# A spectral-mixing kernel with its rows re-tiled so that every output DMA spans 128 partitions, and its last mode split over two PSUM banks

## The chip, the core and the metric

The kernel runs on one core of a Trainium2 chip. A core has five engines that run side by side: TensorE (PE, with weight loads, PEld, shown apart), VectorE (DVE), ScalarE (ACT), GpSimd (POOL) and SyncE (SP), and 16 DMA engines that move data between HBM and the on-chip memory SBUF. SBUF and PSUM, where matmuls accumulate, have 128 partitions. The metric is the device time of one execution in microseconds; lower is better.

## What is computed

Linear attention over 8 batches, 8 heads, 576 rows and head size 64, then a mixing of the rows in the Fourier domain with one pair of 512x512 weight matrices for each of 64 modes, and a channel product with a ReLU:

```python
def phi(x):  return np.where(x > 0, x, np.exp(x) - 1.0) + 1.0
q_p, k_p = phi(q), phi(k)
kv  = np.einsum('bhsd,bhse->bhde', k_p, v)
num = np.einsum('bhsd,bhde->bhse', q_p, kv)
den = np.einsum('bhsd,bhd->bhs', q_p, np.sum(k_p, axis=2))[..., None] + 1e-06
x   = (num / den).transpose(0, 2, 1, 3).reshape(B, S, H * D)   # 8 x 576 x 512

X = np.fft.rfft(x, axis=1)[:, :64]
Y[:, :64] = X * (w_r + 1j * w_i)       # per mode m: a 512x512 complex product
u = x + np.fft.irfft(Y, n=S, axis=1)
out = u + np.maximum(u @ w_ch, 0.0)    # float32
```

The weights are 128 matrices of 1 MB each, so most of the bytes that are read are weights. The output has 8 x 576 x 512 numbers of 4 bytes, 9.44 MB.

## The kernel before

The 576 rows of a batch are cut into four main tiles of 128 rows and a tail of 64; two batches' tails share one tile. Thus there are 36 tiles, t = 0 to 35. The kernel has three stages.

First, for each batch, q, k and v are loaded with a partition holding 9 consecutive rows (s = 9 p + j), phi is applied, and q is transposed on TensorE. The transposes for the nine j go to PSUM in an order that makes four tiles of 128 columns, and ScalarE copies them to `qT`:

```python
for sl in range(NJ):                                    # NJ = 9, NP = 64
    j = 8 if sl == 8 else 4 * (sl % 2) + sl // 2
    nc.tensor.transpose(qT_ps[:, sl]..., phi["q", b][:, hpp, j]..., id16)
nc.scalar.copy(out=qT[:, hpp].rearrange("p t (j r) -> p t j r", r=NP),        # L231
               in_=qT_ps.rearrange("p j t r -> p t j r"))
...
def num_matmuls(num, orow, qT, kv_sb, jj, pinned=False):
    cols = slice(jj * 128, min(jj * 128 + 128, NJ * NP))
    ...  nc.tensor.matmul(num[hpo][orow, c0:c0 + 65],                         # L158
                          qT[rows, hpp, h2, cols], kv_sb[rows, hpp, h2, :])
```

So partition p of tile jj holds row 9 p' + jj (first 64 partitions) or 9 p' + 4 + jj (second 64). The Fourier constants are built for this order. A transform of x gives the modes (L295, weights `x16[:, jj, dc::4]`).

Second, the weights stream in, and each mode is a product over four column groups of the array, a copy out of PSUM, and a pick of the rows (L372):

```python
def mode_product(kk, ps, stage, yt_ps):
    wr, wi = w_get(kk)
    P = ps.tile([128, D], F32, tag="P", bufs=2)
    for dc in range(NDC): nc.tensor.matmul(P[quad, :], xt_cols(dc, 1, kk), wr[:, dc, :], ...)  # L354
    if kk >= NM - 4: keep_warm(6)
    for dc in range(NDC): nc.tensor.matmul(P[quad, :], xt_cols(dc, 0, kk), wi[:, dc, :], ...)  # L362
    st = stage.tile([128, D], F16, tag="ystage", bufs=2)
    (VectorE for even kk, else ScalarE): copy st <- P                                          # L368, L370
    for ec in range(NDC): nc.tensor.matmul(yt_ps[:, ec, kk % 8, :], st[...], pick_sb)          # L372
```

Beside it, `channel_product` forms x again for each tile (L158 once more), and `form_rows` makes Y and Z = Y w_ch for the first 56 modes (L490, L494).

Third, when the last mode is there, Z and y of the last eight modes are formed, sent to the other batches' tiles by small DMAs, and each tile gets its inverse transform (L517), ReLU on ScalarE (L547), the addition on VectorE (L553) and its output DMA:

```python
for ec in range(NDC): nc.tensor.matmul(z_ps, rows[ec], wch16[:, ec, :], ...)      # L603
for ec in range(NDC): nc.tensor.transpose(y_ps[:, ec, :], rows[ec], id16)         # L605
nc.scalar.copy(out=last[:, 1, 0:hw], in_=z_ps[:, 0:hw])                           # L607
nc.vector.tensor_copy(out=last[:, 1, hw:D], in_=z_ps[:, hw:D])                    # L608
nc.vector.tensor_copy(out=last[:, 0, :], in_=y_ps...)                             # L609
for b in range(1, B): eng.dma_start(out=YZ[b][2 * NE:128], in_=last[b::B])        # L612
...
def end(t, acc, single):
    add_inverse(acc, t, 0)
    nc.vector.tensor_tensor(out=x, in0=acc, in1=x, op=ALU.add)                    # L553
    if t < B * NJJ:                                  # a main tile; every second one, or a single one
        ov = out[b].rearrange("(p j) d -> p j d", j=NJ)
        for j2 in range(2):
            (nc.sync, nc.gpsimd)[j2].dma_start(                                   # L560
                out=ov[:, 4 * j2 + j0 : 4 * j2 + jj + 1, :],
                in_=x_main[b][j2 * 64 : j2 * 64 + 64, j0 : jj + 1, :])
    else:                                            # a tail tile: 64 partitions to each of two batches
        for hf in range(2): (nc.sync, nc.gpsimd)[hf].dma_start(...)               # L567
```

Main tiles are written in pairs (4 KB a partition), except the first two and the last two (2 KB). The tiles are worked off in the order of the batches, each pair of batches' tail tile ahead of the last two main tiles of the second batch.

Of the kernel before, what the change touches and what calls it, by code (L numbers as in the profile page):

```python
# [10 lines left out]
F32 = mybir.dt.float32  # L11
F16 = mybir.dt.float16
# [4 lines left out]
NJ = 9  # L17
NP = 64


def _dft_consts(S: int, NM: int, NL: int, NB: int):

    p = np.arange(NP)
    m = np.arange(NM)
    fwd = np.zeros((128, 5, 2 * NM), dtype=np.float64)
    s_cols = np.empty(S, dtype=np.int64)
    for jj in range(4):
        for j2 in range(2):
            s = NJ * p + 4 * j2 + jj
            ang = 2.0 * np.pi * np.outer(s, m) / S  # L30
            fwd[j2 * 64 : j2 * 64 + 64, jj, :NM] = np.cos(ang)
            fwd[j2 * 64 : j2 * 64 + 64, jj, NM:] = -np.sin(ang)
            s_cols[jj * 128 + j2 * 64 + p] = s
    s = NJ * p + 8
    ang = 2.0 * np.pi * np.outer(s, m) / S
    for half in range(2):
        fwd[half * 64 : half * 64 + 64, 4, :NM] = np.cos(ang)
        fwd[half * 64 : half * 64 + 64, 4, NM:] = -np.sin(ang)
    s_cols[512 + p] = s

    scale = np.where(m == 0, 1.0, 2.0) / S
    ang = 2.0 * np.pi * np.outer(m, s_cols) / S
    inv = np.empty((NM, 2, S), dtype=np.float64)
    inv[:, 0, :] = np.cos(ang) * scale[:, None]
    inv[:, 1, :] = -np.sin(ang) * scale[:, None]
    pick = np.zeros((128, 16), dtype=np.float16)
    for quad in range(4):
        for c in range(16):
            pick[quad * 32 + c, c] = 1.0

    inv0 = np.zeros((NL, 2, NB, S), dtype=np.float64)
    inv0[:, :, 0, :] = inv[NM - NL :]
    return (
        fwd.astype(np.float16), inv.reshape(2 * NM, S).astype(np.float16),
        inv0.reshape(2 * NL * NB, S).astype(np.float16), pick,
    )
# [3 lines left out]
def kernel(  # L60
# [10 lines left out]
    nc = tc.nc  # L71

    B, H, S, Dh = q.shape
    D = H * Dh
    NM = moe_w_r.shape[0]
    NHP = H // 2
    NDC = D // 128
    NJJ = 4
# [16 lines left out]
    id16 = const.tile([128, 128], F16, name="id16")  # L95
    fwd_sb = const.tile([128, 5, 2 * NM], F16, name="fwd_sb")
    pick_sb = const.tile([128, 16], F16, name="pick_sb")
    wch16 = const.tile([128, NDC, D], F16, name="wch16")
# [10 lines left out]
    def xt_cols(dc: int, t: int, kk: int):  # L109

        c0 = dc * XDC + t * B * NM + kk
        return xt_c[:, c0 : c0 + 31 * NM + 1 : NM]
# [27 lines left out]
    pin = tc.keep_in_program_order  # L140
# [8 lines left out]
        w_in.setdefault(kk, []).append(w_load(kk, half, pool, tag, bufs))  # L149

    def num_matmuls(num, orow, qT, kv_sb, jj, pinned=False):
        cols = slice(jj * 128, min(jj * 128 + 128, NJ * NP))
        for hpp in range(2):
            for h2 in range(2):
                for hpo in range(2):
                    rows = slice(hpo * 64, hpo * 64 + 64)
                    c0 = (hpp * 2 + h2) * 65
                    mm = nc.tensor.matmul(  # L158
                        num[hpo][orow, c0 : c0 + 65], qT[rows, hpp, h2, cols], kv_sb[rows, hpp, h2, :]
                    )  # L160
                    if pinned:
                        pin(mm)
        return [n[orow, 0:260].rearrange("p (c n) -> p c n", c=4) for n in num]
# [54 lines left out]
    def turn_q(b, hpp):  # L218
        qT = q_view(qT_all[b])
        qT_ps = psA.tile([128, NJ, 2, NP], F16, tag="big", bufs=3, name=f"qTp{b}_{hpp}")  # L220
        for sl in range(NJ):
            j = 8 if sl == 8 else 4 * (sl % 2) + sl // 2
            pin(
                nc.tensor.transpose(  # L224
                    qT_ps[:, sl].rearrange("p t r -> p (t r)"),
                    phi["q", b][:, hpp, j].rearrange("p o d -> p (o d)"),
                    id16,
                )
            )
        pin(  # L230
            nc.scalar.copy(  # L231
                out=qT[:, hpp].rearrange("p t (j r) -> p t j r", r=NP),
                in_=qT_ps.rearrange("p j t r -> p t j r"),
            )
        )

# [106 lines left out]
    def keep_warm(n: int):  # L343

        for _ in range(n):
            nc.tensor.matmul(last_ps[0], id16, wch16[:, 0, :])  # L346

    def mode_product(kk: int, ps, stage, yt_ps):

        wr, wi = w_get(kk)  # L350
        P = ps.tile([128, D], F32, tag="P", bufs=2, name=f"P{kk}")
        for dc in range(NDC):
            quad = slice(dc * 32, dc * 32 + 32)
            nc.tensor.matmul(  # L354
                P[quad, :], xt_cols(dc, 1, kk), wr[:, dc, :],
                start=True, stop=False, tile_position=(0, dc * 32),
            )
        if kk >= NM - 4:
            keep_warm(6)
        for dc in range(NDC):  # L360
            quad = slice(dc * 32, dc * 32 + 32)
            nc.tensor.matmul(  # L362
                P[quad, :], xt_cols(dc, 0, kk), wi[:, dc, :],
                start=False, stop=True, tile_position=(0, dc * 32),
            )
        st = stage.tile([128, D], F16, tag="ystage", bufs=2, name=f"ys{kk}")
        if kk % 2 == 0:
            nc.vector.tensor_copy(out=st, in_=P)  # L368
        else:
            nc.scalar.copy(out=st, in_=P)  # L370
        for ec in range(NDC):
            nc.tensor.matmul(  # L372
                yt_ps[:, ec, kk % 8, :], st[:, ec * 128 : ec * 128 + 128], pick_sb
            )
        if NM - 4 <= kk < NM - 1:
            keep_warm(6)
# [9 lines left out]
    psW = tc.alloc_tile_pool(name="psW", bufs=1, space=bass.MemoryType.PSUM)  # L386
# [23 lines left out]
    for kk in range(n_early):  # L410
# [4 lines left out]
    x_main = [sW.tile([128, NJJ, D], F32, tag="x_main", bufs=B, name=f"x_main{b}") for b in range(B)]  # L415
    x_tail = [
        sW.tile([128, D], F32, tag="x_tail", bufs=B // 2, name=f"x_tail{i}") for i in range(B // 2)
    ]
# [15 lines left out]
    def bank(name: str, shape=(128, D), dtype=F32):  # L434
        return psW.tile(list(shape), dtype, tag="bank", bufs=5, name=name)

    last_ps = []
# [112 lines left out]
    def end(t: int, acc, single: bool):  # L550
        add_inverse(acc, t, 0)
        x = x_of(t)
        nc.vector.tensor_tensor(out=x, in0=acc, in1=x, op=ALU.add)  # L553
        if t < B * NJJ:
            b, jj = divmod(t, NJJ)
            if jj % 2 == 1 or single:
                j0 = jj if single else jj - 1
                ov = out[b].rearrange("(p j) d -> p j d", j=NJ)
                for j2 in range(2):
                    (nc.sync, nc.gpsimd)[j2].dma_start(  # L560
                        out=ov[:, 4 * j2 + j0 : 4 * j2 + jj + 1, :],
                        in_=x_main[b][j2 * 64 : j2 * 64 + 64, j0 : jj + 1, :],
                    )
        else:
            i = t - B * NJJ
            for hf in range(2):
                (nc.sync, nc.gpsimd)[hf].dma_start(  # L567
                    out=out[2 * i + hf].rearrange("(p j) d -> p j d", j=NJ)[:, 8, :],
                    in_=x_tail[i][hf * 64 : hf * 64 + 64, :],
                )  # L570

    order = []
    for i in range(B // 2):
# [8 lines left out]
    for kk in range(n_early, NM):  # L582
        mode(kk)
        want = min(len(tiles), (kk - n_early + 1) * len(tiles) // n_spread)
        while done < want:
            channel_product(tiles[done])
            done += 1
        if kk >= NE - 1:
            while rows_done < min(B, 2 * (kk - NE + 2)):
                form_rows(rows_done)  # L590
                rows_done += 1
        if kk == NM - 5:
            for t in order[:N_PRE]:
                acc = ready[t] = acc_bank(t)
                add_channels(acc, t)
                add_inverse(acc, t, 1, EARLY)
            last_ps += [bank("zl"), bank("ypl", [128, NDC, 128], F16)]


    z_ps, y_ps = last_ps  # L600
    rows = [YT[:, ec, NE:NM, :].rearrange("p m n -> p (m n)") for ec in range(NDC)]
    for ec in range(NDC):
        nc.tensor.matmul(z_ps, rows[ec], wch16[:, ec, :], start=(ec == 0), stop=(ec == NDC - 1))  # L603
    for ec in range(NDC):
        nc.tensor.transpose(y_ps[:, ec, :], rows[ec], id16)  # L605
    hw = D // 2
    nc.scalar.copy(out=last[:, 1, 0:hw], in_=z_ps[:, 0:hw])  # L607
    nc.vector.tensor_copy(out=last[:, 1, hw:D], in_=z_ps[:, hw:D])  # L608
    nc.vector.tensor_copy(out=last[:, 0, :], in_=y_ps.rearrange("p c r -> p (c r)"))  # L609
    for b in range(1, B):  # L610
        eng = nc.sync if b < 3 else nc.gpsimd
        eng.dma_start(out=YZ[b][2 * NE : 128, :, :], in_=last[b::B, :, :])  # L612
# [4 lines left out]
    for n in range(len(order) + SKEW):  # L617
        if n < len(order):
            accs[n] = begin(order[n], ready.get(order[n]))
        if n >= SKEW:  # L620
            t = order[n - SKEW]
# [31 lines left out]
```

## Time and profile before

| what | value |
|---|---|
| median of 3 runs | 437.26 us (436.56 to 438.08) |
| span of the profiled run | 437.0 us |
| PE, DVE, ACT busy | 299.2, 178.3, 148.2 us |
| output written to HBM | 9.44 MB |
| mean granted TensorE clock | 0.714 |

The busy time of an engine is an average over stages that have different limits, so the slices and the stretches of time say more than the totals. In the stretches, each engine's column is its busy time in us with the number of its instructions; then follow the granted clock, the mean busy share of the 16 DMA engines and what they moved. In a time order, the first two columns are the start and the duration in us; SPq is SyncE's issue of a DMA. In the groups of instructions, a row has the line, the engine, the tiles and shapes, the count, the busy time in us and the mean duration in ns.

### The profile page before, as it was taken

The page shows a single profiled execution, that of the slowest core. Times are in us where ns is not written, and L with a number is a line of the kernel's source. Part 1 is how long each engine was busy: PE and PEld are TensorE (multiplying, and loading weights), DVE is VectorE, ACT ScalarE, POOL GpSimd, SP SyncE. Part 2 cuts the span into 40 slices and gives each one's busy share as a digit, 9 for nine tenths or more (in the row PEclk, how much of TensorE's full clock was granted, in tenths as well). Part 3 has the DMA queues.
Part 4 walks back from the last instruction along what each step waited for, and adds up shares of the span by engine and source line. Part 5 has one row for each costly group of instructions (what it writes and reads, how often), then busy time and mean ns, then how long its engine had stood idle before and what let it go on. Part 6 is the DMA issues. An engine that isn't in the chain of part 4 may idle for free.

```text
span 437.0 us, 6270 instructions
## 1 busy us (share of the span) xinstructions
PE 299.2 (68%) x2532; PEld 151.5 (35%) x2532; DVE 178.3 (41%) x350; ACT 148.2 (34%) x227; POOL 102.8 (24%) x185
## 2 busy tenths in 40 slices
PE   0358777786038677686877777878776569988980
PEld 0346555663014232222332223222232229533430
DVE  1699988953004233223223223222232212214980
ACT  3686666621002222222223122222222213104860
POOL 4232322122222122121212112221122211103440
PEclk9996666665559857766557566555666869999995
DMA  8999999999999999999999999999999999992997
GB/s 146 207 208 209 209 209 209 212 214 217 219 213 213 214 213 214 212 214 213 214 214 213 214 213 214 213 214 215 213 213 213 213 214 212 215 181 66 300 319 206
DMA packets 35757, 92.37 MB, mean 211 GB/s; under 512 B 3488, under 2 KB 16672, under 8 KB 35728
## 3 DMA queue, kind: packets, MB, share of 16 engines
q0 software_dynamic: 33328, 86.69, 100.0%
q1 hardware_dynamic: 2400, 5.28, 3.9%
q8 instruction: 20, 0.33, 0.3%
q14 instruction: 9, 0.07, 0.0%
HBM read 164.07 MB, written 9.44 MB: 397 GB/s over the span
## 4 chain that ended last, share of the span: by engine, by line
DMA 66%; PE 13%; issue 9%; DVE 4%; POOL 3%; ACT 2%; POOLq 0%; ACTq 0%; DVEq 0%
DMA wr_1426<-in_moe_w_r_dram 5%; DMA wr_1410<-in_moe_w_r_dram 5%; DMA wr_3557<-in_moe_w_r_dram 4%; DMA wi_2233<-in_moe_w_i_dram 4%; DMA wi_3009<-in_moe_w_i_dram 4%; DMA wr_3409<-in_moe_w_r_dram 4%; DMA wi_2046<-in_moe_w_i_dram 4%; DMA wr_2606<-in_moe_w_r_dram 4%; DMA wr_2446<-in_moe_w_r_dram 4%; DMA wr_3211<-in_moe_w_r_dram 4%; DMA wi_2850<-in_moe_w_i_dram 4%; DMA wi_3812<-in_moe_w_i_dram 4%; DMA k_7_928<-in_k_dram 4%; DMA wi_1829<-in_moe_w_i_dram 4%; DMA k_5_604<-in_k_dram 4%
## 5 line engine op out<-in xcount | busy, mean ns | idle before, releaser
L362 PEld LDWEIGHTS <-xt_c 128*32 128x32 bf16 x256 | 16.4, 161 | 29.0 <-issue 26.3
L354 PEld LDWEIGHTS <-xt_c 128*32 128x32 bf16 x256 | 13.1, 166 | 34.2 <-DMA wr_3493<-in_moe_w_r_dram 3.3
L372 PE MATMUL yt_1445<-pick_sb,ys_1455 128*128 128x16 f16 x4 | 0.3, 174 | 20.3 <-DMA pick_sb<-row_pick 20.3
L517 PEld LDWEIGHTS <-inv_sb 128*128 128x128 f16 (+3 forms) x90 | 7.9, 99 | 11.6 <-issue 5.0
L346 PE MATMUL zl<-wch_67,id_64 128*128 128x512 f16 x42 | 10.6, 380 | 0.0
L368 DVE CAST ys_1485<-P_1476 128x512 f16<-128x512 f32 x1 | 0.7, 692 | 22.8 <-PE P_1476 L362 22.8
L224 PE MATMUL qTp_0_147<-id_64,qe_122 128*128 128x128 f16 x9 | 1.1, 311 | 11.7 <-DVE qe_122 L207 11.7
L370 ACT CAST ys_1500<-P_1491 128x512 f16<-128x512 f32 x1 | 0.6, 586 | 23.0 <-PE P_1491 L362 23.0
L490 PEld LDWEIGHTS <-YT 128*112 128x112 f16 x32 | 7.6, 290 | 1.6 <-issue 1.4
L494 PEld LDWEIGHTS <-YT 128*112 128x112 f16 x32 | 7.4, 293 | 0.2
L372 PEld LDWEIGHTS <-ys_1455 128*128 128x128 f16 x4 | 0.3, 105 | 20.3 <-issue 20.2
L158 PEld LDWEIGHTS <-qT_102 64*128 64x128 f16 (+1 forms) x80 | 2.6, 121 | 10.3 <-ACT qT_102 L231 4.7
L224 PEld LDWEIGHTS <-qe_122 128*128 128x128 f16 x18 | 1.8, 146 | 11.7 <-DVE qe_122 L207 11.7
L536 PEld LDWEIGHTS <-id_64 128*128 128x128 f16 x40 | 3.9, 97 | 5.1 <-issue 2.0
L612 POOL DMA_DIRECT2D YZ_1617<-last x1 | 0.5, 512 | 21.2 <-DVE last L608 21.2
L158 PEld LDWEIGHTS <-qT_107 64*128 64x128 f16 (+1 forms) x80 | 2.7, 122 | 7.1 <-issue 5.2
L158 PEld LDWEIGHTS <-qT_106 64*128 64x128 f16 (+1 forms) x80 | 2.6, 125 | 7.1 <-issue 5.5
L158 PEld LDWEIGHTS <-qT_105 64*128 64x128 f16 (+1 forms) x80 | 2.6, 114 | 7.2 <-issue 6.2
L158 PEld LDWEIGHTS <-qT_108 64*128 64x128 f16 (+1 forms) x80 | 2.3, 113 | 7.2 <-issue 5.7
L346 PEld LDWEIGHTS <-id_64 128*128 128x128 f16 x42 | 3.3, 97 | 4.2 <-issue 1.6
L158 PE MATMUL num_0_223<-kv_75,qT_102 64*128 64x65 f16 x8 | 0.6, 233 | 5.9 <-ACT kv_75 L255 5.9
L158 PEld LDWEIGHTS <-qT_103 64*128 64x128 f16 (+1 forms) x80 | 2.5, 112 | 5.7 <-issue 4.3
(1403 smaller groups left out, 889.4 us busy)
## 6 DMA issues: line engine op xcount, KB each, us to landing
q_0_110<-in_q_dram POOLq DMA_DIRECT2D x1, 576.0 KB, 6.6
k_0_112<-in_k_dram POOLq DMA_DIRECT2D x1, 576.0 KB, 8.6
v_0_114<-in_v_dram POOLq DMA_DIRECT2D x1, 576.0 KB, 10.6
q_1_116<-in_q_dram POOLq DMA_DIRECT2D x1, 576.0 KB, 12.7
k_1_118<-in_k_dram POOLq DMA_DIRECT2D x1, 576.0 KB, 14.8
v_1_120<-in_v_dram POOLq DMA_DIRECT2D x1, 576.0 KB, 17.0
q_2_141<-in_q_dram POOLq DMA_DIRECT2D x1, 576.0 KB, 12.1
k_2_143<-in_k_dram POOLq DMA_DIRECT2D x1, 576.0 KB, 12.0
```

What stands on the lines that cost most here:

```text
L158: mm = nc.tensor.matmul(num[hpo][orow, c0 : c0 + 65], qT[rows, hpp, h2, cols], kv_sb[rows, hpp, h2, :])
L224: nc.tensor.transpose(qT_ps[:, sl].rearrange("p t r -> p (t r)"), phi["q", b][:, hpp, j].rearrange("p o d -> p (o d)"), id16,)
L346: nc.tensor.matmul(last_ps[0], id16, wch16[:, 0, :])
L354: nc.tensor.matmul(P[quad, :], xt_cols(dc, 1, kk), wr[:, dc, :], start=True, stop=False, tile_position=(0, dc * 32),)
L362: nc.tensor.matmul(P[quad, :], xt_cols(dc, 0, kk), wi[:, dc, :], start=False, stop=True, tile_position=(0, dc * 32),)
L368: nc.vector.tensor_copy(out=st, in_=P)
L370: nc.scalar.copy(out=st, in_=P)
L372: nc.tensor.matmul(yt_ps[:, ec, kk % 8, :], st[:, ec * 128 : ec * 128 + 128], pick_sb)
L490: nc.tensor.matmul(z_ps[: 2 * NE, :], lhs[ec], wch16[:, ec, :], start=(ec == 0), stop=(ec == NDC - 1))
L494: nc.tensor.transpose(y_ps[: 2 * NE, ec, :], lhs[ec], id16)
L517: mm = lambda o, l, r: nc.tensor.matmul(o, l, r, start=False, stop=True, skip_group_check=True)
L536: nc.tensor.matmul(acc[:, cols], id16, src, start=(cols.start == 0), stop=False, skip_group_check=True)
```

## The change

The rows are tiled as s = 4 r + jj over the 128 partitions r of tile jj, and the tail holds rows 512 to 575. To this end q's transpose is copied to `qT` in the order of the rows, and a tile takes every fourth column. In HBM, the rows of two neighbouring tiles of one partition lie side by side as before, and now all 128 partitions of a pair of tiles make one regular block, so that one DMA writes it; SyncE and GpSimd take turns. The aim is output DMAs that use the whole width of SBUF. The last mode is computed in two halves of 256 columns in two PSUM banks that are copied out by two engines at once, and Z of the last modes is made in two banks as well, so that copies and matmuls overlap; the copy of y moves from VectorE to ScalarE.

```diff
 def _dft_consts(S, NM, NL, NB):
-    ...  s = NJ * p + 4 * j2 + jj  (rows of tile jj, half j2);  s = NJ * p + 8  (tail)
+    s_cols = np.concatenate([4 * np.arange(128) + jj for jj in range(4)] + [512 + np.arange(NP)])
+    s_rows = np.concatenate([s_cols, s_cols[512:]]).reshape(5, 128).T
+    ...
     def num_matmuls(num, orow, qT, kv_sb, jj, pinned=False):
-        cols = slice(jj * 128, min(jj * 128 + 128, NJ * NP))
+        cols = slice(jj, 512, NJJ) if jj < NJJ else slice(512, NJ * NP)
     def turn_q(b, hpp):
-        for sl in range(NJ):
-            j = 8 if sl == 8 else 4 * (sl % 2) + sl // 2
-            transpose qT_ps[:, sl] <- phi["q", b][:, hpp, j]
+        for j in range(NJ):
+            transpose qT_ps[:, j] <- phi["q", b][:, hpp, j]
         nc.scalar.copy(
-            out=qT[:, hpp].rearrange("p t (j r) -> p t j r", r=NP),
-            in_=qT_ps.rearrange("p j t r -> p t j r"),
+            out=qT[:, hpp].rearrange("p t (r j) -> p t r j", j=NJ),
+            in_=qT_ps.rearrange("p j t r -> p t r j"),
         )
     def mode_product(kk, ps, stage, yt_ps):
+        n_part = 2 if kk == NM - 1 else 1
+        pw = D // n_part
+        P = [ps.tile([128, D], F32, tag="P", bufs=2)[:, 0:pw] for i in range(n_part)]
+        for t, w in ((1, wr), (0, wi)):
+            for i in range(n_part):
+                for dc in range(NDC):  matmul(P[i][quad], xt_cols(dc, t, kk), w[:, dc, i * pw : i * pw + pw])
+        for i in range(n_part):  copy st[:, i * pw : i * pw + pw] <- P[i]   (VectorE if (kk + i) is even, else ScalarE)
     def end(t, acc, single):
-                for j2 in range(2):
-                    (nc.sync, nc.gpsimd)[j2].dma_start(
-                        out=ov[:, 4 * j2 + j0 : 4 * j2 + jj + 1, :],
-                        in_=x_main[b][j2 * 64 : j2 * 64 + 64, j0 : jj + 1, :])
+                queue().dma_start(          # GpSimd, SyncE, GpSimd, ... in turn
+                    out=out[b, 0:512, :].rearrange("(r j) d -> r j d", j=NJJ)[:, j0 : jj + 1, :],
+                    in_=x_main[b][:, j0 : jj + 1, :])
...          (the tail: rows 512 to 575, still 64 partitions to each queue)
-            last_ps += [bank("zl"), bank("ypl", [128, NDC, 128], F16)]
+            last_ps += [bank("zl0"), bank("zl1")]
-    z_ps, y_ps = last_ps
+    y_ps = psW.tile([128, NDC, 128], F16, tag="P", bufs=2, name="ypl")
+    for h in range(2):
+        for ec in range(NDC):  matmul(last_ps[h][:, 0:hw], rows[ec], wch16[:, ec, cols])
+        copy last[:, 1, cols] <- last_ps[h][:, 0:hw]     (ScalarE for h = 0, VectorE for h = 1)
     for ec in range(NDC):  transpose y_ps[:, ec, :] <- rows[ec]
-    nc.vector.tensor_copy(out=last[:, 0, :], in_=y_ps.rearrange("p c r -> p (c r)"))
+    nc.scalar.copy(out=last[:, 0, :], in_=y_ps.rearrange("p c r -> p (c r)"))
```

More of the change, by code (lines that the diff above doesn't have):

```diff
@@ L21, in _dft_consts @@
 def _dft_consts(S: int, NM: int, NL: int, NB: int):
-    p = np.arange(NP)
     m = np.arange(NM)
-    fwd = np.zeros((128, 5, 2 * NM), dtype=np.float64)
-    s_cols = np.empty(S, dtype=np.int64)
-    for jj in range(4):
-        for j2 in range(2):
[L29 to L39, printed above, removed]
+    s_cols = np.concatenate([4 * np.arange(128) + jj for jj in range(4)] + [512 + np.arange(NP)])
+    s_rows = np.concatenate([s_cols, s_cols[512:]]).reshape(5, 128).T
+    ang = 2.0 * np.pi * s_rows[:, :, None] * m / S
+    fwd = np.concatenate([np.cos(ang), -np.sin(ang)], axis=2)
     scale = np.where(m == 0, 1.0, 2.0) / S
@@ L220, in turn_q @@
         qT_ps = psA.tile([128, NJ, 2, NP], F16, tag="big", bufs=3, name=f"qTp{b}_{hpp}")
-        for sl in range(NJ):
-            j = 8 if sl == 8 else 4 * (sl % 2) + sl // 2
+        for j in range(NJ):
             pin(
                 nc.tensor.transpose(
-                    qT_ps[:, sl].rearrange("p t r -> p (t r)"),
+                    qT_ps[:, j].rearrange("p t r -> p (t r)"),
                     phi["q", b][:, hpp, j].rearrange("p o d -> p (o d)"),
@@ L350, in mode_product @@
         wr, wi = w_get(kk)
[L351 to L365, printed above, removed]
-        st = stage.tile([128, D], F16, tag="ystage", bufs=2, name=f"ys{kk}")
[L367 to L370, printed above, removed]
+        st = stage.tile([128, D], F16, tag="ystage", bufs=2, name=f"ys{kk}")
+        n_part = 2 if kk == NM - 1 else 1
+        pw = D // n_part
+        P = [
+            ps.tile([128, D], F32, tag="P", bufs=2, name=f"P{kk}_{i}")[:, 0:pw] for i in range(n_part)
+        ]
+        for t, w in ((1, wr), (0, wi)):
+            for i in range(n_part):
+                for dc in range(NDC):
+                    nc.tensor.matmul(
+                        P[i][dc * 32 : dc * 32 + 32, :], xt_cols(dc, t, kk),
+                        w[:, dc, i * pw : i * pw + pw],
+                        start=(t == 1), stop=(t == 0), tile_position=(0, dc * 32),
+                    )
+            if t == 1 and kk >= NM - 4:
+                keep_warm(6)
+        for i in range(n_part):
+            dst = st[:, i * pw : i * pw + pw]
+            if (kk + i) % 2 == 0:
+                nc.vector.tensor_copy(out=dst, in_=P[i])
+            else:
+                nc.scalar.copy(out=dst, in_=P[i])
         for ec in range(NDC):
@@ L557, in end @@
                 j0 = jj if single else jj - 1
-                ov = out[b].rearrange("(p j) d -> p j d", j=NJ)
-                for j2 in range(2):
-                    (nc.sync, nc.gpsimd)[j2].dma_start(
-                        out=ov[:, 4 * j2 + j0 : 4 * j2 + jj + 1, :],
-                        in_=x_main[b][j2 * 64 : j2 * 64 + 64, j0 : jj + 1, :],
-                    )
+                queue().dma_start(
+                    out=out[b, 0:512, :].rearrange("(r j) d -> r j d", j=NJJ)[:, j0 : jj + 1, :],
+                    in_=x_main[b][:, j0 : jj + 1, :],
+                )
         else:
@@ L567, in end, with queue @@
                 (nc.sync, nc.gpsimd)[hf].dma_start(
-                    out=out[2 * i + hf].rearrange("(p j) d -> p j d", j=NJ)[:, 8, :],
-                    in_=x_tail[i][hf * 64 : hf * 64 + 64, :],
-                )
+                    out=out[2 * i + hf, 512:S, :], in_=x_tail[i][hf * 64 : hf * 64 + 64, :]
+                )
+    n_queue = 0
+    def queue():
+        nonlocal n_queue
+        n_queue += 1
+        return (nc.sync, nc.gpsimd)[n_queue % 2]
     order = []
@@ L596 @@
                 add_inverse(acc, t, 1, EARLY)
-            last_ps += [bank("zl"), bank("ypl", [128, NDC, 128], F16)]
-    z_ps, y_ps = last_ps
+            last_ps += [bank("zl0"), bank("zl1")]
+    y_ps = psW.tile([128, NDC, 128], F16, tag="P", bufs=2, name="ypl")
     rows = [YT[:, ec, NE:NM, :].rearrange("p m n -> p (m n)") for ec in range(NDC)]
-    for ec in range(NDC):
[L603 to L608, printed above, removed]
-    nc.vector.tensor_copy(out=last[:, 0, :], in_=y_ps.rearrange("p c r -> p (c r)"))
+    hw = D // 2
+    for h in range(2):
+        cols = slice(h * hw, h * hw + hw)
+        for ec in range(NDC):
+            pin(
+                nc.tensor.matmul(
+                    last_ps[h][:, 0:hw], rows[ec], wch16[:, ec, cols],
+                    start=(ec == 0), stop=(ec == NDC - 1),
+                )
+            )
+        if h == 0:
+            pin(nc.scalar.copy(out=last[:, 1, cols], in_=last_ps[h][:, 0:hw]))
+        else:
+            pin(nc.vector.tensor_copy(out=last[:, 1, cols], in_=last_ps[h][:, 0:hw]))
+    for ec in range(NDC):
+        pin(nc.tensor.transpose(y_ps[:, ec, :], rows[ec], id16))
+    pin(nc.scalar.copy(out=last[:, 0, :], in_=y_ps.rearrange("p c r -> p (c r)")))
     for b in range(1, B):
```

## The prediction

> **What bounds the kernel now.** I read the slices of the page first, because they show where one limit hands over to the next. The DMA row and the rate row, and then the chain by engine:
>
> ```profile
> DMA  8999999999999999999999999999999999992997
> GB/s 146 207 208 209 209 209 209 212 214 217 219 213 213 214 213 214 212 214 213 214 214 213 214 213 214 213 214 215 213 213 213 213 214 212 215 181 66 300 319 206
> ...
> DMA 66%; PE 13%; issue 9%; DVE 4%; POOL 3%; ACT 2%; POOLq 0%; ACTq 0%; DVEq 0%
> ```
>
> A slice is 437.0 / 40 = 10.9 us. For 35 slices the DMA engines are full with inputs (the rate counts the 2-byte side of a load that reads 4-byte numbers). Slice 37 (393 to 404 us) is nearly empty, and the last three are full again with the output. So there are two DMA-bound stages and a gap: inputs until 394.6 us, where the last weight lands (the first L362 matmul of the last mode starts then), a gap until 401.5 us, where the first output DMA is issued, and output to the end. The busy times by stretch show who is waiting in the last part (columns: PE, PEld, DVE, ACT, POOL busy, clock, DMA share, GB/s):
>
> ```profile
> 396.00:401.00 5.00, 4.61 (x26) 1.77 (x23) 1.23 (x4) 2.15 (x5) 2.28 (x5) 1.00 0.11 33
> 405.00:410.00 5.00, 5.00 (x26) 2.18 (x24) 4.82 (x8) 4.07 (x7) 2.17 (x5) 1.00 0.91 297
> 410.00:415.00 5.00, 5.00 (x26) 2.07 (x23) 4.85 (x8) 4.24 (x8) 2.19 (x5) 1.00 0.94 309
> 415.00:420.00 5.00, 5.00 (x26) 2.01 (x24) 4.66 (x8) 4.08 (x8) 2.17 (x5) 1.00 0.99 327
> 420.00:425.00 5.00, 4.28 (x20) 1.43 (x18) 4.66 (x9) 3.31 (x6) 2.19 (x5) 1.00 0.98 318
> 425.00:430.00 5.00, 0.00 (x0) 0.00 (x0) 0.59 (x1) 0.00 (x0) 1.30 (x3) 0.61 1.00 309
> 430.00:431.00 1.00, 0.00 (x0) 0.00 (x0) 0.00 (x0) 0.00 (x0) 0.00 (x0) 0.50 0.92 279
> 431.00:432.00 1.00, 0.00 (x0) 0.00 (x0) 0.00 (x0) 0.00 (x0) 0.00 (x0) 0.50 0.97 234
> 432.00:436.00 4.00, 0.00 (x0) 0.00 (x0) 0.00 (x0) 0.00 (x0) 0.00 (x0) 0.50 0.55 129
> ```
>
> PE and VectorE work without a pause to 425.6 us, then nothing computes, and the DMA engines drain for 10 us. The time order of the last issues says whose queue drains:
>
> ```profile
> 424.44 3.37 SPq L560 DMA_DIRECT2D out_dram<-x_main_1608  x2
> ...
> 424.90 0.68 DVE L553 TENSOR_TENSOR x_main_1609<-acc_4110,x_main_1609 128x512 f32<-128x512 f32 x1
> 425.28 1.13 POOL L560 DMA_DIRECT2D out_dram<-x_main_1609  x2
> 427.90 1.93 SPq L560 DMA_DIRECT2D out_dram<-x_main_1609  x1
> 429.92 2.12 SPq L567 DMA_DIRECT2D out_dram<-x_tail_1613  x1
> 432.14 1.80 SPq L560 DMA_DIRECT2D out_dram<-x_main_1609  x2
> ```
>
> GpSimd has issued all its halves (partitions 64 to 127) by 426.4 us. SyncE needs 1.8 to 2.1 us an issue here where its first took 0.47 to 0.57, and it puts out its last only at 434 us. From 430.5 us the stream is SyncE's alone, partitions 0 to 63: 0.88 MB between 430.5 and 435.5 us, 176 GB/s. In the trace's DMA packets a 4 KB output packet takes 159 ns at the median and hardly less at best. Between 403.5 and 430.5 us 64% are at that floor and the mean is 201 ns (16 engines x 4096 / 201 = 326 GB/s); after 431 us the mean is 270 ns and 17% are at the floor. An engine that is alone with its packet needs 159 ns: 16 x 4096 / 159 = 412 GB/s.
>
> **What the Trainium skill says.** "SBUF — State Buffer", section "Door 1: The DMA port swizzle", says that partitions 0 to 63 reach only the even 8 of 16 DMA ports and 64 to 127 the odd ones, so a 64-partition transfer tops out at about 218 GB/s. The trace agrees roughly: 129 to 234 GB/s while only SyncE's halves are left. The section "Can I just issue two DMAs to hit both halves?" gives 6% for two halves together; here the trace differs, with 297 to 327 GB/s while both are in flight, and the measurement decides. "DMA: Bandwidth & Descriptors", "The descriptor swizzle", says that a 128-partition transfer gives each engine a port of its own. No run here shows that yet; it is what the change rests on. For the cost side, "TensorE: Matmul & The Clock Gate", "Weight-path perf modes", says that the fast weight load stays on for a strided read of 128 two-byte columns. The trace agrees:
>
> ```profile
> L490 PEld LDWEIGHTS <-YT 128*112 128x112 f16 x32 | 7.6, 290 | 1.6 <-issue 1.4
> ...
> L158 PEld LDWEIGHTS <-qT_107 64*128 64x128 f16 x64 | 2.0, 121 | 6.7 <-issue 4.8 <-ACT qT_107 L231 1.8
> ...
> L224 PEld LDWEIGHTS <-qe_215 128*128 128x128 f16 x18 | 1.8, 147 | 0.1
> ...
> L295 PEld LDWEIGHTS <-x_2_522 128*128 128x128 f16 x16 | 1.4, 136 | 0.4
> ```
>
> L295 loads with a step of 4 elements at 136 ns, L224 without a step at 147; only 112 columns (L490) are dear.
>
> **Part 1, the row tiling up to the output.** The Fourier constants only change their values. The qT copy (L231, 16 times, 1.10 to 1.14 us) now reads PSUM with a 256-byte step and writes in order. I have no row for such a read. Were it twice as slow, each batch would have 2 x 1.1 = 2.2 us more of ScalarE, which is busy 13 to 16 of 20 us in this stage. The weight loads of L158 (some 640, 64x128) get a step of 4 elements; by L295 that costs nothing. Even if it cost as much as L490 against L158 (170 ns), the 36 channel products would have 8 x 0.17 = 1.4 us more each, 49 us over some 250 us in which PE is busy 76%: just still fitting. And delay is not time: input DMAs are issued well ahead. At the narrowest place a weight lands 9.9 us after its issue, where 512 KB take 2.45 us of the stream, so four loads are queued. I put 0 us for this part.
>
> **Part 2, the last mode and Z in two banks.** Now: matmuls 394.60, ScalarE copy of 128x512 0.59 us, pick matmuls, YT copy at 396.10, Z at 396.38 for 1.04 us, transposes to 397.81, and copies until 398.43; the wide inverse matmuls (L517) begin at 398.80. After: the P halves are copied side by side (0.37 us for 128x256 on ScalarE as in L607, 0.41 on VectorE as in L608), which saves 0.2 us. The first half of Z is copied while the second is computed, but the copy of y moves to ScalarE (some 0.55 us) and ends where VectorE's ended, so Z's inverse can start about 0.7 us earlier and y's, with the YZ DMAs, only about 0.2. The instruction order after the change also shows work of the fourth and fifth tile (four matmuls of 0.22) that filled the gaps before and now stands behind them. Each tile needs 3 x 0.216 us on PE and 0.69 on VectorE, so 36 tiles take 36 x 0.69 = 24.8 us from the first addition (400.75) on. I count 0.3 us at the front, and the last addition ends at 425.3 instead of 425.6.
>
> **Part 3, the output DMAs.** 28 halves of pairs of tiles and 8 of single tiles become 18 transfers over 128 partitions (4 KB in one piece in both cases), which alternate between SyncE and GpSimd; the eight 64-partition tail transfers stay. By queue it is 4.7 MB each, as before. What goes is the collision: two engines on one port, and a queue of even ports left over. The stream begins at about 401.7 us. At 412 GB/s, 9.44 MB take 22.9 us, quicker than the tiles are made, and VectorE is the bound: last addition 425.3, issue 0.5, first byte and 256 KB in 0.65, about 427.1 for the last data. At 369 GB/s, halfway between 326 and 412, it is 401.7 + 25.6 = 427.3. From the last data (435.5) to the end (437.0) it is 1.5 us now. So the span becomes 428.6 to 428.8 if the floor of the packets is half or wholly reached. I do not expect all of it (tail halves, transfers of 512 KB that come in lumps, HBM), and take a quarter of the way, 350 GB/s: 401.7 + 27.0 = 428.7, plus 1.5 = 430.2. The time before is 0.2 above the span, within the spread of its runs.
>
> **The rivals.** (a) The rate of 326 GB/s is not set by SBUF ports but on the HBM side. For it: 300 to 327 GB/s whatever the mix of queues. Against it: 64% of packets run at 159 ns while others need twice that, and packets slow down when fewer bytes flow after 431 us. Then only the uneven drain goes: 401.7 + 9.44 / 0.326 = 430.7, plus 1.5 = 432.2. (b) The output rows now lie 8 KB apart in HBM (18 KB before), half of each 8 KB per transfer; if this collides in HBM, the rate may fall to 290 GB/s: 401.7 + 32.6 + 1.5 = 435.8, a wash. Nothing in the profile speaks for it. (c) The strided copy or weight loads turn the input stage PE- or ScalarE-bound: 440 us and more. Against it: L295 and the queue depth. (d) All of it works and the front gains more than I count: 428.0 to 428.5.
>
> **Range and chances.** I give (a) 25%, (b) 7%, (c) 3%, the rest to the main line with (d). Point 430.2, range 428.2 to 433.6. Faster by over 2% means under 428.5, which needs the floor rate and a front gain together: 14%. Slower by over 2% needs (c) or a bad (b): 2%.
>
> **What would show it.** Right: the DMA share of the tail falls while GB/s rises to 350 or more; the mean 4 KB packet falls from 201 towards 165 ns; SyncE's issues stay near 0.5 us; both queues end within 1 us of each other, 2 to 3 us after the last addition. L158 loads stay at 100 to 125 ns. Wrong: 64% of packets or fewer at the floor with full ports (rival a or b), weights landing with PE or ScalarE in front of the DMA chain (c), or a last addition later than 425.6.

## The result and the profile after

| | before | after |
|---|---|---|
| median time | 437.21 us (4 runs) | 433.87 us (4 runs, 433.17 to 434.67) |
| ratio, 95% interval | 1 | 0.9923 (0.9898 to 0.9948) |
| profiled execution: its time | 438.93 us | 433.70 us |
| its span | 437.04 us | 431.49 us |
| last addition ends | 425.59 us | 424.58 us |
| last output data lands | 435.51 us | 429.17 us |
| mean 4 KB output packet after 402 us | 204 ns | 167 ns |

The kernel became 0.8% faster, 3.3 us, where 7.1 us were predicted; 433.87 lies 0.3 us above the predicted range. First the slices of the page of the kernel after (10.8 us each):

```profile
DMA  9999999999999999999999999999999999993796
GB/s 151 208 208 209 209 209 209 212 213 218 218 212 213 214 214 213 213 214 214 213 213 213 214 215 213 214 213 213 213 213 213 214 214 213 213 213 70 283 347 263
```

The input slices are as before, and the first matmul on the last weight starts at 394.05 us where it started at 394.60: the new row tiling costs nothing there. The output slices changed from 300, 319, 206 to 283, 347, 263 GB/s. The stretches of the last part (columns as in the prediction: PE, PEld, DVE, ACT, POOL busy, clock, DMA share, GB/s):

```profile
405.00:410.00 5.00, 5.00 (x26) 2.02 (x25) 4.79 (x8) 4.31 (x8) 1.52 (x3) 1.00 0.86 320
410.00:415.00 5.00, 5.00 (x27) 2.20 (x26) 4.69 (x8) 4.19 (x8) 1.16 (x2) 1.00 0.96 352
415.00:420.00 5.00, 5.00 (x25) 2.10 (x24) 4.85 (x8) 4.21 (x8) 1.68 (x3) 1.00 0.98 354
420.00:425.00 5.00, 3.28 (x16) 0.94 (x14) 4.24 (x7) 2.37 (x5) 1.68 (x3) 1.00 0.98 388
425.00:430.00 5.00, 0.00 (x0) 0.00 (x0) 0.00 (x0) 0.00 (x0) 0.00 (x0) 0.80 0.64 222
```

From 415 to 425 us, at a DMA share of 0.98 to 0.99 in both kernels, the stream now moves 354 to 388 GB/s where it moved 318 to 327: each engine gets more done, not more of its time. After 425 us, data flow for 4.2 us more and not for 10.5. The time order of the last issues (start, duration, engine):

```profile
422.57 0.33 SPq L548 DMA_DIRECT2D out_dram<-x_main_1609  x1
...
423.90 0.68 DVE L543 TENSOR_TENSOR x_main_1609<-acc_4109,x_main_1609 128x512 f32<-128x512 f32 x1
424.28 0.59 POOL L548 DMA_DIRECT2D out_dram<-x_main_1609  x1
424.61 0.63 SPq L548 DMA_DIRECT2D out_dram<-x_main_1609  x1
```

SyncE's issues take 0.33 to 0.63 us, no longer 1.8 to 2.1, and both queues have issued all within 0.7 us of the last addition's end. The last data of GpSimd's DMAs (428.77 us) and of SyncE's (429.17) are 0.4 us apart. The groups of weight loads, by shape, show the strided read (L146 was L158):

```profile
L480 PEld LDWEIGHTS <-YT 128*112 128x112 f16 x32 | 7.8, 291 | 1.8 <-issue 1.4
L146 PEld LDWEIGHTS <-qT_107 64*128 64x128 f16 x64 | 1.9, 118 | 5.9 <-issue 4.4 <-ACT qT_107 L218 1.1 <-DVE x_5_1008 L265 0.4
```

The same tile took 121 ns before. Over the eight batches L158 took 101 to 121 ns, 110 on average, and L146 takes 118 to 125, 122 on average: a strided load is some 12 ns longer, and nothing of it shows in the time of the input stage. The `qT` copy (L218, was L231) stays at 1.10 to 1.14 us although it reads PSUM with a 256-byte step.

### The profile page after: what moved, and what is told of

It is laid out like the page before. It is cut to its first block, busy times and chain, and to the rows that moved or that the text cites. A ratio compares the mean times of both kernels' runs of the same rounds, so it can differ in the third digit from the quotient of the medians.

```text
span 431.5 us, 6261 instructions
## 1 busy us (share of the span) xinstructions
PE 296.4 (69%) x2544; PEld 153.4 (36%) x2544; DVE 178.7 (41%) x350; ACT 148.8 (34%) x228; POOL 97.8 (23%) x176
## 3 DMA queue, kind: packets, MB, share of 16 engines
HBM read 164.07 MB, written 9.44 MB: 402 GB/s over the span
## 5 line engine op out<-in xcount | busy, mean ns | idle before, releaser
L348 PEld LDWEIGHTS <-xt_c 128*32 128x32 bf16 x520 | 25.0, 164 | 64.8 <-issue 27.6
L333 PE MATMUL zl_3714<-wch_67,id_64 128*128 128x512 f16 x42 | 10.6, 380 | 0.0
L146 PEld LDWEIGHTS <-qT_102 64*128 64x128 f16 (+1 forms) x80 | 2.8, 129 | 10.2 <-ACT qT_102 L218 4.7
L146 PEld LDWEIGHTS <-qT_105 64*128 64x128 f16 (+1 forms) x80 | 3.0, 129 | 7.9 <-issue 6.5
L146 PEld LDWEIGHTS <-qT_106 64*128 64x128 f16 (+1 forms) x80 | 2.6, 125 | 6.8 <-issue 4.8
L146 PEld LDWEIGHTS <-qT_108 64*128 64x128 f16 (+1 forms) x80 | 2.5, 124 | 6.7 <-issue 5.2
L146 PE MATMUL num_0_223<-kv_75,qT_102 64*128 64x65 f16 x8 | 0.6, 233 | 5.9 <-ACT kv_75 L242 5.9
L146 PEld LDWEIGHTS <-qT_107 64*128 64x128 f16 (+1 forms) x80 | 2.4, 120 | 6.2 <-issue 4.6
L146 PEld LDWEIGHTS <-qT_103 64*128 64x128 f16 (+1 forms) x80 | 2.9, 128 | 4.4 <-issue 3.8
L146 PEld LDWEIGHTS <-qT_104 64*128 64x128 f16 (+1 forms) x80 | 2.4, 121 | 5.4 <-issue 4.2
```

Source lines behind the costliest of these rows:

```text
L146: mm = nc.tensor.matmul(num[hpo][orow, c0 : c0 + 65], qT[rows, hpp, h2, cols], kv_sb[rows, hpp, h2, :])
L348: nc.tensor.matmul(P[i][dc * 32 : dc * 32 + 32, :], xt_cols(dc, t, kk), w[:, dc, i * pw : i * pw + pw], start=(t == 1), stop=(t == 0), til ...
```

## The experiments

Two theories stood first. *Width*: the gain comes from the output DMAs that span all partitions, and the prediction sized it too large. *Last mode*: much of the gain comes from the front, and the DMAs brought little. A third question came up from the profile after: the last data land 4.6 us after the last addition, although the packets are near the 159 ns of one that is alone. Ratios are to the kernel before on the same chip (its medians there 436.40 to 436.69 us), with 95% intervals.

| run | kernel | median us | ratio | last addition to last data, data to end of span |
|---|---|---|---|---|
| e1_split_out | after, DMAs in halves | 436.55 | 1.000 (0.9991 to 1.001) | 7.31, 1.70 |
| e2_old_last | after, old last mode | 434.38 | 0.9948 (0.9934 to 0.9962) | 4.55, 2.47 |
| e3_tail128 | after, wide tails | 433.41 | 0.9922 (0.991 to 0.9935) | 3.86, 1.87 |
| e4_pitch18 | e3 with an 18 KB pitch | 432.98 | 0.9913 (0.99 to 0.9927) | 3.80, 1.86 |
| e5_after | after itself | 433.95 | 0.9936 (0.9922 to 0.9951) | 5.13, 1.99 |
| e6_fetch_moved | after, 100 small matmuls first | 433.98 | 0.9941 (0.9924 to 0.9958) | 4.85, 2.19 |
| e7_all_sync | after, output all from SyncE | 431.69 | 0.9885 (0.987 to 0.9901) | 3.88, 1.46 |
| e8_only_last | before, new last mode | 436.26 | 0.999 (0.9977 to 1.0003) | 7.69, 1.50 |
| e9_all_sync_again | e7 itself | 431.63 | 0.9895 (0.9879 to 0.991) | 3.44, 1.30 |
| e10_sync_fetch | e7, 80 small matmuls first | 431.32 | 0.9886 (0.9868 to 0.9904) | 3.09, 1.47 |
| e11_all_gpsimd | after, output all from GpSimd | 435.12 | 0.9969 (0.996 to 0.9978) | 5.59, 2.87 |
| e12_sync_fetch_first | e10, six single tiles first | 432.62 | 0.9914 (0.99 to 0.9928) | 3.07, 2.09 |

### Halves again (e1_split_out)

```diff
-    queue().dma_start(out=ov[:, j0 : jj + 1, :], in_=x_main[b][:, j0 : jj + 1, :])
+    for hf in range(2):
+        (nc.sync, nc.gpsimd)[hf].dma_start(
+            out=ov[hf * 64 : hf * 64 + 64, j0 : jj + 1, :],
+            in_=x_main[b][hf * 64 : hf * 64 + 64, j0 : jj + 1, :])
```

> The changed kernel with each main output DMA cut into two again, partitions 0 to 63 on SyncE and 64 to 127 on GpSimd; tiling, last mode and all else as changed. If the width of the output DMAs is what gained (port theory): 4 KB packets back to a mean near 200 ns, 300 to 327 GB/s in the tail, and 436.5 us. If the new row order in HBM or the last mode gained: it stays at 433.9 us and packets near 165 ns.

The whole gain is gone: 1.000. The stretches of this kernel:

```profile
405.00:410.00 5.00, 5.00 (x26) 2.20 (x25) 4.82 (x8) 4.07 (x7) 2.17 (x5) 1.00 0.93 301
410.00:415.00 5.00, 5.00 (x25) 2.11 (x24) 4.85 (x8) 4.17 (x8) 2.18 (x5) 1.00 1.01 367
415.00:420.00 5.00, 5.00 (x26) 2.02 (x25) 4.67 (x8) 4.09 (x8) 2.17 (x5) 1.00 0.95 320
420.00:425.00 5.00, 4.36 (x21) 1.43 (x19) 4.67 (x9) 3.38 (x6) 2.18 (x5) 1.00 1.00 326
425.00:430.00 5.00, 0.00 (x0) 0.00 (x0) 0.66 (x2) 0.00 (x0) 1.37 (x3) 0.79 1.00 333
```

One stretch, 410 to 415 us, reaches 367 GB/s, so single stretches of 5 us scatter. The 20 us from 405 to 425 us together, in the kernel before, in e1 and in the kernel after:

```profile
405.00:425.00 20.00, 19.28 (x92) 7.69 (x89) 18.99 (x30) 15.71 (x27) 8.72 (x17) 1.00 0.96 313
405.00:425.00 20.00, 19.36 (x92) 7.76 (x90) 19.00 (x30) 15.71 (x27) 8.71 (x17) 1.00 0.97 329
405.00:425.00 20.00, 18.28 (x87) 7.27 (x85) 18.57 (x29) 15.08 (x26) 6.03 (x11) 1.00 0.95 353
```

The rate divided by the share is what full engines would move: 326, 339 and 372 GB/s. With the rows of the new tiling but 64 partitions a DMA, a 4 KB packet takes 195 ns in the mean against 167. Where the rows lie in HBM is not the cause: that is the same as in the kernel after. But e1 differs in more than the width, because each pair of tiles is again two DMAs, on two queues at once. In e9 below, where all output comes from SyncE, the 2 KB packets show the width by itself: 89 ns in the mean for the first two single tiles, written over 128 partitions, and 149, 124 and 121 ns for the first three tail tiles, written in two halves of 64.

### The last mode alone, and all but it (e8_only_last, e2_old_last)

e8 is the kernel before with only the two-bank last mode and Z, and y's copy on ScalarE; e2 is the kernel after with the old code for them. The edit (for e2; e8 is the inverse):

```diff
-    n_part = 2 if kk == NM - 1 else 1        # P in two halves, two banks, two copies
+    P = ps.tile([128, D], F32, tag="P", bufs=2)
-    last_ps += [bank("zl0"), bank("zl1")]
+    last_ps += [bank("zl"), bank("ypl", [128, NDC, 128], F16)]
```

> The kernel before with the last mode, Z and the copy of y as changed; tiling and output DMAs as before. If the narrow output stream sets the end: the last addition 0.5 us sooner after the last weight, but the stream ends as late, 436.3 to 436.8 us. If the front sets the end: 435.5 us.

> The changed kernel with the last mode, Z and the copy of y as before; tiling and output DMAs as changed. Port theory: this part is worth 0.3 us at the front and most of that is hidden because the output stream is full at the end, so 434.0 to 434.2 us. Rival (the front is the gain: the first addition came 1.2 us sooner after the last weight): 435.1 us or more.

e8 gives 0.999 with an interval that holds 1; e2 keeps nearly the whole gain, and its interval overlaps that of e5. So this part is worth 0.4 us by the medians, which can't be told from nothing. In the profiles, the last addition ends 30.53 us after the first matmul on the last weight in the kernel after and in e8, and 30.98 us after it in the kernel before and in e2: the new last mode saves 0.45 us at the front, and the medians do not show whether the end keeps it.

### The tails and the pitch (e3_tail128, e4_pitch18)

Both write the output rows in another order than the reference's (the same bytes), so that a tail tile can go out in one DMA over 128 partitions. In e3 the main rows of a partition lie 8 KB apart, as in the kernel after; in e4 they lie 18 KB apart, as in the kernel before.

```diff
-    for hf in range(2): (nc.sync, nc.gpsimd)[hf].dma_start(
-        out=out[2 * i + hf, 512:S, :], in_=x_tail[i][hf * 64 : hf * 64 + 64, :])
+    queue().dma_start(out=flat[4096 + i * 128 : 4096 + i * 128 + 128, :], in_=x_tail[i])   # e3
+    queue().dma_start(out=blk[:, NJ - 1, :], in_=x_tail[i])                                 # e4
```

> The changed kernel with the tail tiles, too, written by one DMA over 128 partitions; rows go to other places of the output (main tiles first, tails behind), with the same bytes. If the eight 64-partition tail transfers keep the stream below the floor rate: 2 KB packets of the tails from about 155 to 85 ns, 380 to 400 GB/s from 410 to 425 us, and some 1.5 us less, 432.4 us. If HBM or the queues limit: 433.9 us and no more than 355 GB/s.

> As the run with 128-partition tails, but rows of neighbouring partitions lie 18 KB apart in HBM as in the kernel before, not 8 KB (permuted output, same bytes). If the 8 KB step collides in HBM: at least 1 us faster than the run with 128-partition tails. If the step does not matter: within 0.5 us of it.

The 2 KB packets of the tails fell from about 155 ns to 90, and the last data come 0.7 to 1.3 us sooner after the last addition than in the two profiles of the kernel after. But the stream reaches 364 to 369 GB/s between 410 and 425 us, not the 380 to 400 expected, and the interval of e3 overlaps that of e5: the medians differ by 0.5 us (433.41 against 433.95) where 1.5 were expected, and how much is gained at all stays unclear. e4 and e3 are 0.4 us apart with overlapping intervals: no effect of the pitch shows.

### The kernel after once more, and instruction fetch (e5_after, e6_fetch_moved)

In the kernel after, one 16 KB transfer of TensorE's instructions (the trace has 20 for some 5,100 instructions of TensorE, each some 0.9 us on one DMA engine) falls at 418 us, into the output. The idea: that engine lags, and the last DMAs wait for it. e6 puts 100 matmuls of 16 columns ahead of everything, so that another instruction number stands at that time.

```diff
+    idle = psA.tile([128, 2, 512], F32, tag="big", bufs=3)
+    for _ in range(100): nc.tensor.matmul(idle[:, 0, 0:16], id16, id16[:, 0:16])
     load(0)
```

> The changed kernel itself, as the control for the runs beside it: ratio 0.992, span 431.6 us and 2.2 us beyond the span.

> The changed kernel with 100 tiny matmuls (16 columns, on the identity) while TensorE waits for its first data. They move the fetch of TensorE's instructions (one 16 KB transfer of 0.9 us on one DMA engine) from 418 us, in the full output stream, to the empty stretch near 397 us. If the engine that does this fetch falls behind and ends last (the landings of one transfer spread over 1.3 to 2.5 us from then on): spread back near 0.2 us until 424 us and the last data 1 to 1.5 us sooner after the last addition, about 432.4 us. If the fetch does not matter: as the control, within 0.4 us.

The fetch moved from 418 to 399 us, and the time did not: 433.98 against 433.95. The first half of the idea holds. Of the transfers that SyncE issues at 417 and 418 us, the 16 engines' landings lie 1.9 to 2.0 us apart in e5 and 0.5 to 0.6 in e6. But in e6, too, those of the last two transfers lie 1.7 to 1.9 us apart, and the last data come 4.85 us after the last addition (4.6 and 5.1 in the two profiles with the fetch at its old place). In e6's profile the last addition itself comes 0.4 us later after the last weight than in e5's, which may hide a gain of that size, but not the 1 to 1.5 us expected. The idea is refuted as the cause of the late end.

### One queue (e7_all_sync, e9_all_sync_again, e11_all_gpsimd)

```diff
-    return (nc.sync, nc.gpsimd)[n_queue % 2]
+    return nc.sync                                  # e7, e9; nc.gpsimd in e11; the tails likewise
```

> The changed kernel with every output DMA on SyncE, none on GpSimd. If GpSimd's drain, which ended 1.5 us after its own last landing, holds up the end: from the last data to the end 1.5 us instead of 2.3, and 433.1 us. If two queues are needed to fill the 16 DMA engines: under 330 GB/s in the tail and 435 us or more.

> The changed kernel with every output DMA on SyncE, once more, as the control for the runs beside it: 431.7 us, ratio 0.9885.

> Every output DMA on GpSimd. If two queues in turn are what spreads the 16 engines apart: the spread of a transfer's landings at the end is under 0.6 us as with SyncE alone, the last data come 3.9 us after the last addition, and only the end is later (GpSimd's drain, 2.3 us or more after the last data): 432.7 us. If GpSimd's transfers are the slow ones: spread 1.3 us or more and 434 us or more.

All output from SyncE: 431.7 and 431.6 us, 2.3 less than the kernel after. All from GpSimd: 435.1, 1.2 more. So it is not the use of two queues in turn that costs (then both should gain), but GpSimd's. For e7, 433.1 was expected, from a shorter end alone. In the profiles of e5 and e7 the end is 0.5 us shorter, and the time from the last addition to the last data 1.2. The stretches of e9, then of e11:

```profile
405.00:425.00 20.00, 18.17 (x87) 7.21 (x84) 18.46 (x29) 14.97 (x26) 0.00 (x0) 1.00 0.98 366
410.00:415.00 5.00, 5.00 (x25) 2.17 (x24) 4.80 (x8) 4.19 (x8) 0.00 (x0) 1.00 1.00 373
415.00:420.00 5.00, 5.00 (x24) 2.08 (x23) 4.85 (x8) 4.15 (x9) 0.00 (x0) 1.00 0.95 349
420.00:425.00 5.00, 3.17 (x15) 0.94 (x13) 4.13 (x7) 2.33 (x4) 0.00 (x0) 1.00 1.01 399
425.00:430.00 5.00, 0.00 (x0) 0.00 (x0) 0.00 (x0) 0.00 (x0) 0.00 (x0) 0.77 0.43 152
```

```profile
405.00:425.00 20.00, 18.19 (x87) 7.22 (x84) 18.48 (x29) 15.00 (x26) 11.01 (x21) 1.00 0.95 351
410.00:415.00 5.00, 5.00 (x25) 2.18 (x24) 4.78 (x8) 4.19 (x8) 2.81 (x6) 1.00 0.91 321
415.00:420.00 5.00, 5.00 (x25) 2.08 (x23) 4.85 (x8) 4.17 (x8) 2.75 (x6) 1.00 1.01 379
420.00:425.00 5.00, 3.19 (x15) 0.94 (x13) 4.16 (x7) 2.33 (x4) 2.95 (x6) 1.00 0.97 370
425.00:430.00 5.00, 0.00 (x0) 0.00 (x0) 0.00 (x0) 0.00 (x0) 0.81 (x2) 0.50 0.75 261
```

PE and VectorE do the same work to within 0.03 us (last additions at 424.5 us in both). From 405 to 425 us the engines are busy for 0.98 of the time with SyncE and for 0.95 with GpSimd, at nearly the same rate when full (373 and 369 GB/s). After 425 us SyncE's stream needs 0.43 of a stretch and GpSimd's 0.75. The list of DMA issues of e9, then of e11 (tiles, issuing queue, KB each, median us from issue to landing):

```profile
out_dram<-x_main SPq DMA_DIRECT2D x14, 512.0 KB, 3.0
```

```profile
out_dram<-x_main POOLq DMA_DIRECT2D x14, 512.0 KB, 4.3
```

The packets are hardly slower (4 KB: 161 ns in the median against 159; the means, 177 and 162, do not compare, because e11 writes the tails, too, in 4 KB packets, e9 in packets of 2 KB), yet a transfer lands 1.3 us later. The Trainium skill, "DMA: Bandwidth & Descriptors", section "SWDGE vs HWDGE vs iDMA", says that a DMA issued from GpSimd has its descriptors written by software, one issued from SyncE by hardware, and that a plain transfer belongs on SyncE or ScalarE; "Latency and other measured facts" on the same page gives about 1 us to the first byte for the former and 0.6 for the latter. The traces agree in direction: 1.2 us from the first output issue to its first data in e11, 0.9 in e9, and GpSimd begins its issue 0.26 us later after the same addition. That is half a microsecond, of which 0.3 are part of the 1.3. The rest comes between first data and last landing.

The 16 engines' landings of each of the last two transfers lie 1.3 to 1.9 us apart in the kernel after, e5 and e11, and 0.3 to 0.8 in e7, e9 and e10. (With wide tails, e3 and e4, it is 0.8 to 0.9 although GpSimd issues every second transfer.) At the program's end the long DRAIN instruction with which GpSimd ends finishes 1.6 to 2.1 us after its last data (after 430.41 against 428.77 us, e5 431.22 against 429.66, e11 432.16 against 430.08), and the span ends about 1 us later. With SyncE alone, the span ends 1.3 to 1.5 us after the last data. Why GpSimd's landings spread and its drain takes so long, no run here shows.

### Two attempts on top of one queue (e10_sync_fetch, e12_sync_fetch_first)

In the profile of e7 the 16 KB instruction fetch at 418 us was followed by a microsecond with only two of 16 engines busy. e10 moves it to 401 us by 80 small matmuls at the start. e12 also writes the first six main tiles singly, so that the stream starts with smaller lumps.

```diff
+    for _ in range(80): nc.tensor.matmul(idle[:, 0, 0:16], id16, id16[:, 0:16])   # e10, e12
-    single = set(order[:2] + order[-2:])
+    single = set(order[:6] + order[-2:])                                          # e12
```

> Every output DMA on SyncE and 80 tiny matmuls while TensorE waits for its first data, which move its instruction fetch from about 418 to about 403 us. With one queue the fetch cost a whole gap: at 419 us only 2 of 16 DMA engines were busy for 1 us, and SyncE's issue took 1.77 us. If the queue waits for the one engine that fetches, and at 403 us there is slack to catch up: 0.8 to 1.0 us less than the control, 430.8 us. If the gap has another cause: as the control.

> As the run with SyncE alone and the moved fetch, and the first six main tiles written one by one (256 KB) instead of in pairs. Between 401 and 405 us about a quarter of the DMA engines' time is empty because a pair waits for its second tile. If the stream is the bound from its start: 0.5 to 0.8 us less than that run, 430.2 us. If the tiles are made no faster than they are written: no change.

e10 gives 431.32 against 431.63: the intervals overlap. In e9's profile, the same kernel as e7, 13 of 16 engines were busy in the microsecond that had two in e7, so a gap of that depth is not in every execution, and no clear gain from moving the fetch shows. Again it only brings the landings together: those of the two tail halves issued at 417 to 418 us lie 0.2 and 0.6 us apart in e10, 2.1 and 1.9 in e9. e12 was to gain and is 1.3 us slower than e10. From last addition to last data it takes the same 3.07 us; the end takes 0.6 us longer, and its last weight landed 0.5 us later. Why is open.

## Why the prediction missed, point by point

**The mechanism was right.** The DMAs over 64 partitions held the stream back: packets went from 204 to 167 ns, the width makes the gain (gone in e1, absent in e8, and the packets of e9 show the width by itself), SyncE's issues became short, both queues end together, and the DMA stretch in which only partitions 0 to 63 were left is gone. One sign did not come: the DMA share of the stream was to fall, and is 0.95 from 405 to 425 us where it was 0.96. Rival (a), a limit of 326 GB/s at HBM, is refuted by 399 GB/s in e9. Rival (b), the pitch, shows no effect in e4. Rival (c) is refuted: the copy is as before, the strided weight loads are only 12 ns longer, and a weight lands 10.1 us after its issue at the narrowest place (9.9 before). Part 1 at 0 us was right. Part 2 was put at 0.3 us and is 0.45 in the profile.

**The sum was not.** It said: last data at 428.7, plus 1.5 to the end of the span, 430.2, and that was taken for the time. The profiled execution of the kernel after has 429.17, plus 2.32, plus 2.21 from span to time: 433.70. The three terms are off by 0.5, 0.8 and 2.2 us, together 3.5.

- *"The time before is 0.2 above the span, within the spread of its runs."* This is the step that failed. It set the span of one execution (437.0) against the median of others (437.26). The execution that was profiled took 438.93 us itself, 1.9 above its span, and was longer than any of the timed runs. In the runs of the kernel before beside the experiments, the time is 2.0 us above the span in the median, and the median span is 434.6. The kernel after has 2.2, so this is an addend (2.0 to 2.6 in the medians of all kernels here) that nearly cancels in a difference, but not where the new span is worked out absolutely and then read as a time. The same execution also seems to have had an unusually long drain: 9.9 us from the last addition, where e1 and e8, kernels with the same halves and the same time as before, have 7.3 and 7.7 in theirs. (The kernel before itself has no second profile.) If theirs is the usual drain, the gain that could be had there was some 2.4 us smaller than the profile let it seem. Worked out as a difference from such a drain, 7.5 to the 3.4 predicted, with 0.3 at the front, the gain would have been 4.4 us, and 432.9 us the forecast: within the range, though that is hindsight.
- *"From the last data (435.5) to the end (437.0) it is 1.5 us now."* It is 2.3 in the kernel after and 2.0 in e5. Before, GpSimd's long drain ended at 432.52 us, 3 us ahead of SyncE's last data, and was hidden; now both queues end together and the drain shows. In e7 and e9, without GpSimd's DMAs, it is 1.3 to 1.5.
- *"I do not expect all of it ... take a quarter of the way, 350 GB/s."* The packets did better (167 ns would be 392 GB/s of full engines), the stream worse: 9.44 MB from 400.3 to 429.2 us are 327 GB/s. The engines were not always full: the shares from 405 to 425 us (0.86, 0.96, 0.98, 0.98) leave 1.1 us of them empty, 400 to 405 us, when tiles are only starting, leaves 1.4 (shares by the microsecond 0.23, 0.84, 0.63, 0.88, 1.01), and the last 4.2 us leave 1.0. The stream also began 1.4 us sooner than the 401.7 assumed, so its end is off by just 0.5. *"Both queues end ... 2 to 3 us after the last addition"* was thus wrong, 4.6 us; with SyncE alone it is 3.1 to 3.9 (e7, e9, e10).

So of the 7 us predicted some 2 were never there: 437.0 us is the span of an execution that was 2.4 us longer than the median span of 434.6, and it happened to lie near the usual time, so that a new span could pass for a new time. About 2 more are there but were not had, because half of the DMAs stayed on GpSimd. e7 and e9 show the latter: 431.6 to 431.7 us, ratio 0.9885 to 0.9895, faster than both kernels.

## What to carry to other kernels

Write a profile's prediction as a difference between two spans, and ask first whether the profiled execution's own time is typical: a drain that is some 2 us longer than the usual one is worth more than half of a change of this size. Where the output stream sets the end, let each DMA span all 128 partitions, and issue it from SyncE rather than GpSimd (tried here for all output DMAs, not for the last ones alone). A wait that is removed shows the next one that it hid: here the end of GpSimd's queue.

## What the runs showed of the hardware

- Two concurrent 64-partition streams on two queues do not add up to one over 128 partitions: from 405 to 425 us, 313 and 329 GB/s (before and e1) against 353 and 366 (after and e9), at DMA shares of 0.95 to 0.98. On one queue, 2 KB packets of 64-partition transfers took 121 to 149 ns in the mean, of 128-partition transfers 89 (e9).
- Which engine issues the output is worth 3.5 us at the end of this program: 435.12 us all from GpSimd, 431.63 all from SyncE.
- One output stream to HBM from one core reached 399 GB/s over 5 us (e9), near 16 engines at the 159 ns of a packet alone.
- A weight load of 64x128 with a step of four 2-byte numbers took 122 ns on average where one in order took 110. A ScalarE read of PSUM with a 256-byte step took the 1.10 to 1.14 us of one in order.
- A 16 KB fetch of TensorE's instructions holds one DMA engine for 0.9 us, and the landings of a transfer then in flight spread over 2 us instead of 0.5 (e5 against e6), without an effect on the time (433.95 against 433.98 us).
